# Transposing one more step by DMA, each transposition in two transfers, in a linear-attention and MLP kernel

## The chip, the cores and the metric

The kernel runs on one core of a Trainium2 chip. The metric is the device time of one execution in microseconds. Before the change it is 198.24 us, the median of three runs (198.15 to 199.05). The engines are named as in the profile: PE (TensorE, matrix products), PEld (its weight loads), DVE (VectorE), ACT (ScalarE), POOL (GpSimd) and SP (SyncE, which issues nearly all DMAs here; SPq is its queue of instructions).

## The reference

A lightning attention (linear attention with a decay `lam` per head) over 4 batches, 8 heads, 768 positions and head size 64, followed by a two-layer MLP with a tanh GELU (3072 tokens, 512 to 2048 to 512).

```python
for b in range(nb):                       # blocks of 64 positions
    intra = einsum('bhic,bhjc->bhij', qb, kb) * Dmask      # decayed causal mask
    intra = einsum('bhij,bhjd->bhid', intra, vb)
    inter = einsum('bhid,bhde->bhie', qb * lam_pow, kv_state)
    out[:, :, sl] = intra + inter
    kv_state = lam_block * kv_state + einsum('bhsd,bhse->bhde', kb * rev_pow, vb)
x = out.transpose(0, 2, 1, 3).reshape(3072, 512)
h = x @ w_in
g = gelu_tanh(h)
return g @ w_out
```

## The kernel before

**Steps.** The attention is cut into 24 steps. A step is one batch, one stretch of 256 positions and one half of the heads (four), so steps 2n and 2n + 1 are the two head halves of the same positions. For each step the kernel does the following, in functions that take the step's number:

- `load_step` (L60) issues the loads of q, k and v from HBM, 256 KB each, on SP (L70). The buffers rotate by four, so step n uses those of step n - 4.
- `cast_q` (L277) scales q by its decay into half precision on DVE (L282); `cast_k` (L290) casts k on ACT (L295); both write one tile `qk16`. `scale_v` (L264) scales v on POOL (L266). `prep_qk` is the casts and then `transpose_dma`; `prep` is `prep_qk` and then `prep_v`, which also issues loads for later steps.
- The scores need q and k with the head size on the partitions, so `qk16` is transposed into `qkT`. `FIRST_DMA_T` (L39) is 8. For steps below it `stage_t` (L309) transposes on PE (L321, eight instructions into one PSUM tile `Tps`), and ACT (L328, steps 5 and 6) or DVE (L330, steps 4 and 7) copies the result out. From step 8 on `transpose_dma` (L299) issues one transposing DMA on SP (L303) over queries and keys together, and `stage_t` returns at once.
- `scores` (L344) multiplies queries and keys on PE (L350); `causal` (L356) applies the mask on DVE (L360). `products` (L365) makes the products of keys and values of step n and the attention outputs of an earlier step s. `R(n, s)` (L967) is scores of n, products, mask and the first half of the state update; `U(n)` is the second half. `update` (L535) makes t on DVE (L547, L550) and u on POOL (L558, L565), and a later step's outputs read u.
- From step 13 on two steps at a time go through `burst` (L437).

**The MLP** follows in seven groups of positions. Its pieces are put in a list, `filler`, and `fill(n)` takes the next n pieces into PE's order. A piece is four or eight matrix products, of Hps (L613, first layer) or of MX, MY and MW (L692). The second layer uses sums of weight and activation blocks to save products; the sums of activations, gs (L662), are made on DVE behind the pieces that `queue_group` chose for them. The outputs of the MLP are put together on DVE (L734, L740), ACT (L714) and POOL (L749) and stored to HBM. The outputs of group 0 are kept in two tiles `o_pairs`, each stored by `store_pair` (L591) with two transfers on SP (L594). These tiles and the output tile of group 2 share two rotating buffers (tag `o32`), so that of group 2, first written at L734, takes over the buffer of pair 0.

**Order.** Every engine works its instructions off in the order in which the program names them (`pin`). The end of the function (from L993) is that order written out by hand, for all engines at once. A DMA waits on SP for its data and its buffer, and everything behind it on SP waits too. The change lies in the part from step 6 to step 12:

```python
    fill(1); prep(8); fill(1)            # L1076 to L1078
    stage_t(7)                           # L1079
    sum_wout(1, 4, DVE)
    fill(2)
    R(7, 6, lambda: prep_qk(9))          # L1082
    store_pair(0)
    U(7)
    scale_v(9)
    fill(2)
```

The loads run ahead of this: steps 0 to 8 are loaded by the opening of the function, step 9 by `prep(6)`, q and k of step 10 by `prep(7)`, step 11 by `prep(8)`, and v of step 10 behind step 9's transposition. The loop over `FILL` (L1088) then treats steps 8 to 12: in turn n it casts and transposes step n + 2 and issues the loads of later steps.

Of the kernel before, what the change touches and what calls it, by code (L numbers as in the profile page):

```python
# [15 lines left out]
def kernel(  # L16
# [10 lines left out]
    nc = tc.nc  # L27
    pin = tc.keep_in_program_order
# [7 lines left out]
    NF = DFF // P  # L36
    NC = DM // P
    NSTEP = B * NSB * 2
    FIRST_DMA_T = 8  # L39
    PSUM = bass.MemoryType.PSUM  # L40

    const = ctx.enter_context(tc.tile_pool(name="const", bufs=1))
# [17 lines left out]
    def load_step(s, names="qkv"):  # L60
        b, r = divmod(s, 2 * NSB)
        sb, half = divmod(r, 2)
        ts = ld32.setdefault(s, [])
        for nm, src in (("q", q), ("k", k), ("v", v)):
            if nm not in names:
                continue
            t = ld.tile([P, HH, 2, D], FP32, tag=nm + "32", name=f"{nm}32_{s}")
            rows = src[b, half * HH : (half + 1) * HH, sb * SB : (sb + 1) * SB, :]
            queue = nc.scalar if (nm, s) == ("v", 0) else nc.sync
            pin(queue.dma_start(out=t[:].rearrange("p h j d -> p h (j d)"),  # L70
                                in_=rows.rearrange("h (p j) d -> p h (j d)", j=2)))
            ts.append(t)
# [49 lines left out]
    def sum_wout(j, m, eng):  # L122

        a, op, b = W_SUMS[m]
        r = slice(4 * j, 4 * j + 4)

        def rows(t):
            if t in w_slot:
                return w_sum16[:, w_slot[t], r, :]
            f, e = t  # L130
            return w_out16[:, f * HF + r.start : f * HF + r.stop, e * HE : e * HE + HE]

        pin(eng.tensor_tensor(rows(m), rows(a), rows(b), op))
# [36 lines left out]
    def load_ahead(s):  # L170
        if s < NSTEP:
            load_step(s)
# [72 lines left out]
    def prep(s):  # L245
        prep_qk(s)
        prep_v(s)

    def wide(t):
        return t.rearrange("p j h d -> p h j d")  # L250

    def decay(t, s):
        hs = halves[s % 2]
        return t[:, hs, :].unsqueeze(3).to_broadcast([P, HH, 2, D])

    def prep_v(s):
        scale_v(s)
        if s >= 6:
            if s + 3 == FIRST_DMA_T + 2:
                load_step(s + 3, "qk")  # L260
            else:
                load_ahead(s + 3)

    def scale_v(s):  # L264
        tv = a16p.tile([P, 2, HH, D], FP16, tag="v16", name=f"v16_{s}")
        pin(nc.gpsimd.tensor_tensor(wide(tv[:]), ld32[s][2][:], decay(dv, s), ALU.mult))  # L266
        a16[s] = a16[s] + (tv,)

    def prep_qk(s):
        cast_qk(s)  # L270
        transpose_dma(s)

    def cast_qk(s):
        cast_q(s)
        cast_k(s)

    def cast_q(s):  # L277
        q32 = ld32[s][0]
        tqk = a16p.tile([P, 2, 2, HH, D], FP16, tag="qk16", name=f"qk16_{s}")
        tq, tk = tqk[:, 0], tqk[:, 1]  # L280
        q_eng = nc.gpsimd if s == 3 else nc.vector
        pin(q_eng.tensor_tensor(wide(tq), q32[:], decay(dq, s), ALU.mult))  # L282
        if s == 0:
            inverse(halves[0])
            odd(halves[1])
            inverse(halves[1])
        a16[s] = (tq, tk)
        whole_qk[s] = tqk
# [10 lines left out]
    def transpose_dma(s):  # L299
        tqk = whole_qk.pop(s)  # L300
        if s >= FIRST_DMA_T:
            o = qkp.tile([P, 2, 2, 2, P], FP16, tag="qkT", name=f"qkT_{s}")
            pin(nc.sync.dma_start_transpose(out=o[:].rearrange("p a j h t -> p (a j h) t"),  # L303
                                            in_=tqk[:].rearrange("p a j h d -> p (a j h d)")))
            qkT[s] = o
            if s == FIRST_DMA_T + 1:
                load_step(s + 1, "v")

    def stage_t(s):  # L309
        if s >= FIRST_DMA_T:  # L310
            return
        tq, tk = a16[s][:2]
        if s < 4:
            Tps = [ps_M.tile([P, 2, 2, P], FP16, tag="M", name=f"Tps{i}") for i in range(2)]
        else:
            Tps = ps_M.tile([P, 2, 2, 2, P], FP16, tag="M", name="Tps")
        for i, t in enumerate((tq, tk)):
            to = Tps[i] if s < 4 else Tps[:, i]
            for hp in range(2):
                for j in range(2):  # L320
                    pin(nc.tensor.transpose(to[:, j, hp, :], t[:, j, 2 * hp : 2 * hp + 2, :],  # L321
                                            ident[:]))
        o = qkp.tile([P, 2, 2, 2, P], FP16, tag="qkT", name=f"qkT_{s}")
        if s < 4:
            pin(nc.scalar.activation(out=o[:, 0], in_=Tps[0][:], func=AF.Copy))
            pin(nc.vector.tensor_copy(out=o[:, 1], in_=Tps[1][:]))
        elif s in (5, 6, 8):
            pin(nc.scalar.activation(out=o[:], in_=Tps[:], func=AF.Copy))  # L328
        else:
            pin(nc.vector.tensor_copy(out=o[:], in_=Tps[:]))  # L330
        qkT[s] = o
# [12 lines left out]
    def scores(n):  # L344
        o = qkT[n]
        Sps = [ps_M.tile([P, 2, 2, P], FP32, tag="M", name=f"S{hl}") for hl in range(2)]
        for hp in range(2):
            for jk in range(2):
                for hl, c in TILES:
                    pin(nc.tensor.matmul(  # L350
                        Sps[hl][half64(c), hp, jk, :], o[half64(hl), 1, jk, hp, half64(c)],
                        o[half64(hl), 0, :, hp, half64(c)], start=True, stop=True,
                        skip_group_check=True))
        Ss[n] = Sps

    def causal(n):  # L356

        t = ptp.tile([P, 2, 2, 2, P], FP16, tag="PT", name=f"PT_{n}")
        for hl, Sps in enumerate(Ss.pop(n)):
            pin(nc.vector.tensor_tensor(  # L360
                t[:, hl].rearrange("p b c d -> p b (c d)"), Sps[:].rearrange("p b c d -> p b (c d)"),
                mask[:].unsqueeze(1).to_broadcast([P, 2, 2 * P]), ALU.mult))
        PTs[n] = t
# [227 lines left out]
    def store_pair(pair):  # L591
        rows = out[2 * pair * P : 2 * pair * P + 2 * P, :].rearrange("(i p) d -> p i d", p=P)
        for i in range(2):
            pin(nc.sync.dma_start(out=rows[:, i], in_=o_pairs[pair][:, i]))  # L594
# [368 lines left out]
    def fill(n):  # L963
        for _ in range(min(n, len(filler))):
            filler.pop(0)()

    def R(n, s, ahead=None, keep=False):  # L967

        def first():
            if n is not None:  # L970
                scores(n)
            if ahead:
                ahead()

        if s in NARROW:
            products(n, s, between=first)
        else:
            first()
            products(n, s)
        if n is not None:  # L980
            causal(n)
        if s is not None and s % 2 == 1:
            g, i = group_of[s // 2]
            if i == len(groups[g]) - 1 and g > 0:
                queue_group(g)
        if n is not None and not keep:
            update(n, 0)

    def U(n):
        update(n, 1)  # L990
# [8 lines left out]
    R(0, None)  # L999
    idle(0, 384)  # L1000
    stage_t(1)
    idle(3)
    U(0)
# [72 lines left out]
    fill(1)  # L1076
    prep(8)
    fill(1)  # L1078
    stage_t(7)  # L1079
    sum_wout(1, 4, DVE)  # L1080
    fill(2)
    R(7, 6, lambda: prep_qk(9))  # L1082
    store_pair(0)
    U(7)
    scale_v(9)
    fill(2)

    FILL = {8: (2, 0, 0, 0), 9: (1, 2, 1, 2), 10: (0, 1, 1, 3), 11: (0, 1, 1, 3), 12: (0, 2, 1, 3)}  # L1088
    for n, (a, b, c, d) in FILL.items():
        stage_t(n)  # L1090
        fill(a + (n == 10))
        if n == 8:
            cast_q(n + 2)
            fill(1)
            cast_k(n + 2)
            transpose_dma(n + 2)
        else:
            prep_qk(n + 2)
        if n < 11:
            load_step(n + 4, "qkv" if n < 10 else "qk")  # L1100
        if n == 11:
            scale_v(13)
            load_step(14, "v")
            load_step(16, "qk")
        elif n == 9:
            scale_v(11)
        elif n == 10:
            scale_v(12)
            load_step(15, "qk")
        elif n == 12:  # L1110
            scale_v(14)
        fill(b + (n == 8) - (n == 10))
        R(n, n - 1, keep=n == 8)
        fill(c)
        if n == 8:
            update(n, 0)
            scale_v(n + 2)
            fill(2)
        U(n)
        if n == 12:  # L1120
            prep_qk(15)
            load_step(15, "v")
            load_step(16, "v")
            scale_v(15)
        fill(d)
        if n > 8:
            sum_win((n - 7) // 2, (n - 1) % 2, nc.vector)
# [40 lines left out]
    fill(1)  # L1168
    prep_qk(21)
    prep_v(20)  # L1170
    fill(3)

# [52 lines left out]
```

## Time and profile before

| what | value |
|---|---|
| time, median of three runs | 198.24 us (198.15 to 199.05) |
| profiled execution: its time, and its span | 198.35 us, 196.5 us |
| granted clock of PE | 1.000 |
| DVE busy | 145.7 us (74%) |
| DMA engines, busy share, 0 to 126 us | full or nearly in most slices |
| DMA_TRANSPOSE on SP | 16, of 1.23 to 3.36 us each on SP; 4.1 to 6.0 us from issue to landing, median 4.6 |
| loads of q, k and v | 256 KB each, median 4.9, 5.1 and 5.3 us from issue to landing |

The span runs from the first to the last instruction. The table of DMA issues gives the time from the start of an issue on SP to the landing of the last byte. In the chain of waits a piece is one stretch of equal instructions with its start, its length and its count; matrix products are pipelined, so lengths in the chain are counted up to the start of the next piece. In the timeline of SP a row is the issue of a DMA, not its transfer; the transfer goes on after it.

### The profile page before, as it was taken

The numbers are of one execution on the slowest core, as the hardware profiler recorded it, in microseconds if no ns is written. First come the engines' busy times: TensorE is split into PE (matmuls) and PEld (weight loads), VectorE is DVE, ScalarE is ACT, GpSimd is POOL, SyncE is SP. The second block draws the span as 40 slices with busy tenths as digits, with TensorE's granted clock in tenths as the row PEclk, the third lists the DMA queues.
The fourth block names the chain that finished last, engine by engine and source line by source line (L and its number), as shares of the span: only waits on it lengthen the run. The fifth ranks groups of instructions, "written<-read, shape, count | busy, mean of one in ns | idle before, by whom it ended". The sixth has DMA issues, their size and how long they took to land.

```text
span 196.5 us, 5993 instructions
## 1 busy us (share of the span) xinstructions
PE 190.4 (97%) x2467; PEld 139.2 (71%) x2469; DVE 145.7 (74%) x291; ACT 125.7 (64%) x248; POOL 68.5 (35%) x85
## 2 busy tenths in 40 slices
PE   8979999999999999999999999999999999999993
PEld 2556544456888888754688754578888888888882
DVE  4897722888989879959989826999557996487620
ACT  3663878358774796676856379844877856679221
POOL 6594213457444832528523416064002030002000
PEclk9999999999999999999999999999999999999999
DMA  5999999999999999989999999900520300020205
GB/s 166 291 323 385 384 385 386 302 293 276 267 218 239 262 199 220 239 137 220 361 240 273 251 333 164 227 6 0 36 95 32 110 5 0 3 107 31 79 15 198
DMA packets 62810, 38.13 MB, mean 194 GB/s; under 512 B 18624, under 2 KB 55744, under 8 KB 62784
## 3 DMA queue, kind: packets, MB, share of 16 engines
q1 hardware_dynamic: 62240, 37.50, 76.1%
q8 instruction: 19, 0.31, 0.6%
q10 hardware_dynamic: 544, 0.26, 0.5%
q14 instruction: 7, 0.06, 0.1%
HBM read 27.26 MB, written 6.29 MB: 171 GB/s over the span
## 4 chain that ended last, share of the span: by engine, by line
PE 89%; SPq 4%; DMA 4%; ACT 0%; issue 0%
PE Hps L613 25%; PE MX L692 18%; PE MY L692 9%; PE HX L796 7%; PE O2ps L628 7%; PE MW L692 4%; DMA wi<-in_moe_w_in_dram 4%; SPq L70 4%; PE HY L796 4%; PE S L350 3%; PE Hps L895 3%; PE HW L796 2%; PE O L460 1%; PE OK L400 1%; PE Tps L321 1%; PE OK L422 1%
## 5 line engine op out<-in xcount | busy, mean ns | idle before, releaser
L613 PE MATMUL Hps<-xT,w_in 128*128 128x512 f16 (+1 forms) x288 | 50.5, 332 | 0.0
L613 PEld LDWEIGHTS <-w_in 128*128 128x128 f16 x288 | 27.8, 98 | 19.4
L617 ACT ACTIVATE gT<-Hps 128x512 f16<-128x512 f32 x56 | 32.6, 597 | 9.2 <-PE Hps L613 8.7
L360 DVE TENSOR_TENSOR PT<-S,mask 128x512 f16<-128x512 f32 x48 | 30.3, 681 | 8.8 <-PE S L350 8.8
L266 POOL TENSOR_TENSOR v<-v,dv 128x512 f16<-128x512 f32 x24 | 27.4, 1147 | 19.9 <-DMA v<-in_v_dram 11.5
L692 PEld LDWEIGHTS <-gs 128*128 128x128 f16 x320 | 31.1, 98 | 3.7
L692 PEld LDWEIGHTS <-gT 128*128 128x128 f16 x240 | 23.1, 98 | 3.5 <-ACT gT L617 0.2
L565 POOL TENSOR_TENSOR u<-t,lumask 128x256 f16<-128x256 f32 x21 | 15.6, 758 | 22.1 <-DVE t L550 13.0
L692 PE MATMUL MX<-w_sum,gs 128*128 128x256 f16 x160 | 21.4, 273 | 0.0
L295 ACT ACTIVATE qk<-k 128x512 f16<-128x512 f32 x23 | 14.4, 625 | 7.3 <-DMA k<-in_k_dram 7.1
L282 DVE TENSOR_TENSOR qk<-q,dq 128x512 f16<-128x512 f32 x23 | 17.9, 780 | 1.1 <-DMA q<-in_q_dram 1.1
L749 POOL TENSOR_TENSOR o<-u,q 128x512 f32<-128x512 f32 (+1 forms) x5 | 5.6, 1120 | 37.3 <-issue 34.8
L662 DVE TENSOR_TENSOR gs<-gT 128x1024 f16<-128x1024 f16 (+1 forms) x24 | 16.4, 689 | 3.0 <-ACT gT L617 3.0
L558 POOL TENSOR_TENSOR u<-t,lamu 128x128 f16<-128x128 f32 x19 | 11.2, 597 | 18.7 <-DVE t L550 8.9
L628 PE MATMUL O2ps<-w_out,gT 128*128 128x512 f16 x64 | 14.6, 379 | 0.0
L796 PEld LDWEIGHTS <-ws 128*128 128x128 f16 x128 | 12.4, 98 | 1.7 <-DVE xs L775 0.3
L529 ACT ACTIVATE xT<-OK 128x256 f16<-128x256 f32 x22 | 8.7, 454 | 6.4 <-PE OK L413 3.1
L714 ACT ACTIVATE u<-MX 128x256 f32<-128x256 f32 x18 | 6.9, 383 | 7.4 <-PE MX L692 7.4
L628 PEld LDWEIGHTS <-gT 128*128 128x128 f16 x64 | 6.1, 98 | 6.6
L692 PE MATMUL MY<-w_out,gs 128*128 128x256 f16 x80 | 10.7, 273 | 0.0
L810 DVE COPY u<-HX 128x512 f32<-128x512 f32 x8 | 5.5, 689 | 6.8 <-ACT gT L814 4.4
L350 PEld LDWEIGHTS <-qkT 64*64 64x64 f16 x384 | 6.3, 106 | 5.8 <-issue 2.8
(105 smaller groups left out, 328.5 us busy)
## 6 DMA issues: line engine op xcount, KB each, us to landing
q<-in_q_dram SPq DMA_DIRECT2D x24, 256.0 KB, 4.9
k<-in_k_dram SPq DMA_DIRECT2D x24, 256.0 KB, 5.1
v<-in_v_dram SPq DMA_DIRECT2D x23, 256.0 KB, 5.3
out_dram<-o SPq DMA_DIRECT2D x23, 256.0 KB, 4.5
wo<-in_moe_w_out_dram SPq DMA_DIRECT2D x4, 1024.0 KB, 9.5
wi<-in_moe_w_in_dram SPq DMA_DIRECT2D x4, 512.0 KB, 8.1
wi<-in_moe_w_in_dram SPq DMA_DIRECT2D x2, 1024.0 KB, 13.8
v<-in_v_dram ACTq DMA_DIRECT2D x1, 256.0 KB, 4.3
```

The source lines that it names most:

```text
L266: pin(nc.gpsimd.tensor_tensor(wide(tv[:]), ld32[s][2][:], decay(dv, s), ALU.mult))
L282: pin(q_eng.tensor_tensor(wide(tq), q32[:], decay(dq, s), ALU.mult))
L295: pin(nc.scalar.activation(out=wide(tk), in_=k32[:], func=AF.Copy))
L350: pin(nc.tensor.matmul(Sps[hl][half64(c), hp, jk, :], o[half64(hl), 1, jk, hp, half64(c)], o[half64(hl), 0, :, hp, half64(c)], start=True, ...
L360: pin(nc.vector.tensor_tensor(t[:, hl].rearrange("p b c d -> p b (c d)"), Sps[:].rearrange("p b c d -> p b (c d)"), mask[:].unsqueeze(1).t ...
L565: pin(nc.gpsimd.tensor_tensor(u[:], state[half][:].unsqueeze(2).to_broadcast([P, 2, 2, D]), lumask[:, 2 * half : 2 * half + 2, :].unsqueez ...
L613: pin(nc.tensor.matmul(by_block(Hps[:, i, :]), w_in16[:, c, f * P : (f + 1) * P], x(c), start=(c == 0), stop=(c == NC - 1)))
L617: pin(nc.scalar.activation(out=dst, in_=Hps[:], func=AF.Gelu_apprx_tanh))
L628: pin(nc.tensor.matmul(O2[tau][0][:], gT[:, f % HF, f // HF, tau * P : (tau + 1) * P], w_out16[:, f, :], start=(n == 0), stop=(n == NF - 1)))
L662: pin(nc.vector.tensor_tensor(g_rows(m, i), g_rows(a, i), g_rows(b, i), op))
L692: pin(nc.tensor.matmul(dst, lhsT, rhs, start=(opens and i == 0), stop=(closes and i == HF - 1), skip_group_check=True))
L796: pin(nc.tensor.matmul(dst[:, i, :], w_in_block(a, slice(c, c + 1), slice(f * P, f * P + P))[:, 0], x_block(b, slice(c, c + 1))[:, 0], sta ...
```

## The change

Step 7 is transposed by DMA, too. Each transposition by DMA is two transfers, one of queries and one of keys. Step 9's loads are issued behind step 7's transposition, and q and k of step 10 and all of step 11 behind step 8's. Step 9 is cast behind update 7 instead of inside R(7, 6), and one fill piece goes from behind update 7 to ahead of R(7, 6). `store_pair(0)` is issued behind step 12's transposition. In turn 8 of the loop one fill piece goes from behind the key cast of step 10 to ahead of it.

```diff
-    FIRST_DMA_T = 8
+    FIRST_DMA_T = 7
...
     def prep_v(s):
         scale_v(s)
-        if s >= 6:
-            if s + 3 == FIRST_DMA_T + 2:
-                load_step(s + 3, "qk")
-            else:
-                load_ahead(s + 3)
+        if s == 8:
+            load_step(s + 2, "qk")
+        if s > 7:
+            load_ahead(s + 3)
...
             o = qkp.tile([P, 2, 2, 2, P], FP16, tag="qkT", name=f"qkT_{s}")
-            pin(nc.sync.dma_start_transpose(out=o[:].rearrange("p a j h t -> p (a j h) t"),
-                                            in_=tqk[:].rearrange("p a j h d -> p (a j h d)")))
+            for a in range(2):
+                pin(nc.sync.dma_start_transpose(out=o[:, a].rearrange("p j h t -> p (j h) t"),
+                                                in_=tqk[:, a].rearrange("p j h d -> p (j h d)")))
             qkT[s] = o
-            if s == FIRST_DMA_T + 1:
+            if s == 7:
+                load_step(s + 2)
+            elif s == 9:
                 load_step(s + 1, "v")
...
-        elif s in (5, 6, 8):
+        elif s in (5, 6):
             pin(nc.scalar.activation(out=o[:], in_=Tps[:], func=AF.Copy))
...
     prep(8)
     fill(1)
-    stage_t(7)
     sum_wout(1, 4, DVE)
-    fill(2)
-    R(7, 6, lambda: prep_qk(9))
-    store_pair(0)
+    fill(3)
+    R(7, 6)
     U(7)
+    fill(1)
+    prep_qk(9)
     scale_v(9)
-    fill(2)
...
         if n == 8:
             cast_q(n + 2)
-            fill(1)
+            fill(2)
             cast_k(n + 2)
             transpose_dma(n + 2)
         else:
             prep_qk(n + 2)
+        if n == 10:
+            store_pair(0)
         if n < 11:
             load_step(n + 4, "qkv" if n < 10 else "qk")
...
-        fill(b + (n == 8) - (n == 10))
+        fill(b - (n == 10))
         R(n, n - 1, keep=n == 8)
```

## The prediction

> **What bounds the kernel now.** I read the page's busy rows first (PE 97% of a span of 196.5 us, granted clock full in all slices), then the chain that ended last in order of time, then the stretches of 4 to 12 us.
>
> ```profile
> PE 190.4 (97%) x2467; PEld 139.2 (71%) x2469; DVE 145.7 (74%) x291; ACT 125.7 (64%) x248; POOL 68.5 (35%) x85
> ```
>
> The chain around step 7 (start us, us, what):
>
> ```profile
> 49.44 0.87 PE Hps L613 x8
> 50.31 0.45 PE Tps L321 x8
> 50.76 1.75 PE Hps L613 x16
> 52.50 0.35 PE S L350 x16
> ```
>
> Each piece begins where the one before ends: 49.44 + 0.87 = 50.31, and so on. In the stretches from 18.4 to 193.3 us PE is idle for 0.10 us in all. So no stall is left on PE that this change could take away. What it can gain is PE work that disappears; what it can lose is every wait of PE that it creates. The question is therefore how much slack each late operand has.
>
> **What goes.** Step 7's eight transpositions (0.45 us, the second chain row) leave PE and nothing lies beside them there: gain 0.45 us. The copy of the result, a DVE L330 of 0.69 us at 50.79, goes too; DVE is not on the chain there, so I count nothing. The fill pieces around step 7 keep their total of six; one of 0.87 us moves from behind update 7 to ahead of step 7's scores. These therefore start at 52.50 - 0.45 + 0.87 = 52.92, and everything from step 8 on 0.45 earlier (step 8's scores at 58.76 - 0.45 = 58.31). The edit of the copy's engine list for step 8 has no effect, since that step already went by DMA.
>
> **What is added: 18 more transposing DMAs on SP** (17 steps in two halves against 16 whole). The rows of SP's timeline that price them:
>
> ```profile
> 50.81 1.76 SPq L303 DMA_TRANSPOSE qkT<-qk  x1
> 52.63 0.56 SPq L70 DMA_DIRECT2D q<-in_q_dram  x1
> ...
> 83.39 1.23 SPq L303 DMA_TRANSPOSE qkT<-qk  x1
> 84.73 1.28 SPq L70 DMA_DIRECT2D v<-in_v_dram  x1
> ...
> 87.82 1.57 SPq L303 DMA_TRANSPOSE qkT<-qk  x1
> ```
>
> The trace has no half transposition. A whole one takes SP at least 1.23 us, a plain load at best 0.45. Bounds of a half: 0.62 (all of it scales) to 1.23 (none does). I take 0.84 = 0.45 + half of 0.78, so a pair takes 1.68, 0.45 more than one whole. Part of this costs nothing: the load behind step 15's transposition took 1.28 instead of 0.5, because SP was held up by what the transposition had queued, and a longer issue eats out of that hold-up. A gain is possible too: the queries' half waits for DVE alone and may start while ACT still casts the keys.
>
> A rule speaks against the split. The Trainium skill, "DMA: Bandwidth & Descriptors", section "Rules for kernel authors", says to join many small transfers into one large one, and its fit for a DMA (made for the GpSimd path, section "Anatomy of one DMA") has some 2.0 us that don't depend on size. If a second half paid that again in series, an estimate from that page, step 16's transposition would land 2.0 us later and, after the slack below, cost 1.7 us: 199.6. The trace has four loads issued back to back at 71.66, 72.28, 72.83 and 73.38; the first two landed 3.2 and 3.6 us after issue, 1.0 us apart, so the fixed parts overlap. I take the row: no second fixed part.
>
> **Step 7's new path.** Before, SP was free for step 9's loads at 45.89; these now stand behind step 7's transposition. Its query cast on DVE ends at 47.01, the key cast on ACT at 47.72; step 8's transposition began 0.15 us after its casts, so the halves are issued at 47.16 and, behind the first, 48.0. Landing: steps 14 and 15 took 4.1 us from issue with little in flight, steps 9 and 10 5.6 us behind a full queue. From 48.0 that is 52.1 to 53.6, needed at 52.92. The last load in front (v of step 8, issued 45.02, 5.0 to landing) lands at 50.0, and step 8's transposition landed 1.0 us behind its last load (k of step 10, 54.3 to 55.3). That is nearest to the lower end: 52.1 to 52.4, slack 0.5 to 0.8. Cost zero, at worst 0.7.
>
> **What stands behind it.** Loads land 0.85 us apart in this stretch (q and k of step 9: 50.9, 51.7). Between k of step 10 (54.3) and q of step 11 (57.4) lie 3.1 us for one transposition and one load, so a transposition holds the queue for 2.3. The skill's "Advanced Engine Details and Errata", section "X-Bar Transpose (TRN2)", calls transposing DMAs as fast as regular ones; by it step 7 would add 0.85 and q of step 10 would be in time, by the row it is late. I take the row. In order:
> - Step 9's loads are issued at some 49 to 50.6 instead of 45.9 to 48.6. At 5.0 they land from 54.0 on; the cast of q9 now stands behind update 7, at some 55.5. No wait.
> - Step 8's transposition: halves at 50.8 and 51.7, landing 56.2 (4.5 as before) to 57.3 (5.6), needed 58.31. No cost; cover gone only if it took 6.6.
> - q10 is issued at 52.5 instead of 48.67, lands at 57.6; DVE wants it at 57.42 - 0.45 = 56.97. DVE waits 0.6, with g sums and step 8's mask (L360) queued behind it. The g sum behind it began at 58.45 after 0.35 us idle; it now starts 0.28 late. The g sum that PE reads in the product MY of 62.29 ended at 61.73, and its second half is read 0.44 into that product, at 62.73: 1.0 us of slack, 0.7 of it left. Hidden, unless q10 lands after some 58.3; then every 0.1 us costs 0.1, at most 0.6. k10 is cast two fill pieces later than q10, behind a copy that ends at 58.8; it lands at 58.2.
> - Step 9: casts end at about 56.2, halves issued 56.3 and 57.1, landing by 62.7; scores at 64.34 - 0.45 = 63.9. Step 10: second half at 59.6, landed 65.2, needed 68.3. v10 comes 0.6 to 1.5 late; POOL has the update product of step 9 behind it, done by about 66.5 and needed at 68.6.
>
> **The two stores** (0.97 us of SP at 57.96) move from ahead of step 10's transposition to behind step 12's. That frees the queue where it is full. Step 12's casts end at 69.64 - 0.45 = 69.2; its halves leave SP at 71.0 or so, the stores at 72.0. They must land before DVE L734 writes the same output buffer for group 2 (77.50, so 77.05 now). With 3.6 us (the loads of that moment) they land at 75.6, with 5.1 (these stores before) at 77.1. I take the first. If late, DVE L734 holds up the g sum behind it (77.83, ended 78.33), which PE reads half way into the MY product of 78.27, at 78.71: 0.4 us of slack, so even 77.1 costs nothing. Step 14's loads follow 0.5 us late; their casts are at 78.6 and 79.2, landing at 76.
>
> **Step 16 is the narrowest place.** It was issued at 87.82, behind step 15's transposition and four loads, and landed 5.8 later, at 93.62. PE began the scores of steps 15 and 16 at 93.62 and reached step 16's half 0.28 us later. Slack 0.28. SP's chain begins at step 15's cast on DVE, so it moves up by 0.45 with PE. Against that stand step 15's extra issue (0 to 0.45) and step 16's own (0 to 0.45): 0 to 0.9 later, less 0.28 slack, is a stall of 0 to 0.6. Because the load behind had 0.8 us of hold-up to give, I take 0.4, so 0.1 of stall. The others have more: step 15 lands at 87.5 for 93.6, step 17 at 101.7 for 103.4, step 18 at 110.5 for 116.3.
>
> **Sum** on the profiled execution's 198.35 us (span 196.5 and 1.85 around it): 198.35 - 0.45 + 0.1 = 198.0. The median of three is 198.24, 0.11 lower, which would give 197.9; I leave 198.0.
>
> **Rivals.**
> 1. *Operands land late around steps 7 to 10* (queue as full as for step 9). For it: the DMA rows are full until some 65 us, and a transposition of 2.3 us is put in. Against it: slacks of 0.5 to 2. Step 7 0.7 late plus q10 0.3: 198.35 - 0.45 + 1.0 = 198.9. Chance 20%.
> 2. *Slower: the halves cost SP as much as wholes*, 1.23 us each. Place: step 16, with steps 15 and 16 each 1.23 longer, so 2.5 late less 0.28: 2.2 us of PE idle at 93.4. Sum 198.35 - 0.45 + 2.2 = 200.1. It decides from a half of about 1.0 us, where the stall is 1.1 and the time 199.0; past 0.5% from about 1.15 us, or less where rival 1 adds to it. For it: the shortest transpositions all lie at 1.23 to 1.28, as a fixed cost would. Against it: a plain load of the same bytes takes 0.45, so what is more must come from the pieces, which halve. Chance 18%.
> 3. *The copy that leaves DVE frees more than PE's 0.45.* Against it: PE has no idle time there. To be 0.5% faster needs 1.0 us. Chance 2%.
>
> **Chances.** Changes within 0.5% (1.0 us) can't be told from none here. Forecast (197.6 to 198.4) 60%; rival 1 20%, nearly all within 0.5%; rival 2 18%, nearly all past it; rival 3 2%. Faster 0.03, same 0.76, slower 0.21. The range 197.6 to 199.6 leaves out the upper part of rival 2.
>
> **What would show it.** Right: 34 DMA_TRANSPOSE rows of 0.7 to 0.9 us where SP is unhindered; eight Tps L321 fewer; scores of step 7 without idle PE before them; POOL, DVE and ACT waits at 55 to 65 us that nobody on PE waits for. Wrong: PE idle before S L350 at about 53 (rival 1) or 93.4 (rival 2), or before MY L692 at 61 to 62.

## The result and the profile after

The changed kernel takes 203.51 us (median of six, 202.16 to 204.84) against 198.24 (median of six here, 198.15 to 199.05): the ratio is 1.0257, with a 95% interval of 1.0205 to 1.031. It is slower, where the prediction had 198.0 and a range up to 199.6. The profiled execution took 204.84 us, the slowest of the six, with a span of 203.0 us against 196.5 before, so its waits show the places better than the typical sizes. The ratios below leave out executions that took over 1.5% longer than the fastest of their kernel: one of the kernel with a small extra transposition, three of the four with v on ACT, and one of 682.24 us of the kernel split in all steps but 15 and 16.

From the page of the changed kernel, the busy row and the shares of the chain that ended last:

```profile
PE 193.1 (95%) x2461; PEld 139.1 (68%) x2461; DVE 146.2 (72%) x290; ACT 126.9 (62%) x248; POOL 68.8 (34%) x85
...
PE 73%; DMA 16%; SPq 5%; ACT 2%; DVE 1%; issue 1%; ACTq 0%
```

The chain now leaves PE: DMA holds 16% of it, where PE held 89% and DMA 4% before. PE's own timeline names the places. A row is start us, length us, line and operation, and in brackets PE's idle time before it and what ended that:

```profile
62.61 0.61 PE L694 MATMUL MY<-w_out,gs 128*128 128x256 f16 x4 [0.55 <-DVE gs L664]
...
69.94 0.30 PE L415 MATMUL OK<-qkT,u 64*64 64x128 f16 x7 [0.36 <-POOL u L560]
...
78.97 0.61 PE L694 MATMUL MX<-w_sum,gs 128*128 128x256 f16 x4 [0.24 <-DVE gs L664]
...
80.84 0.61 PE L694 MATMUL MY<-w_out,gs 128*128 128x256 f16 x4 [0.82 <-DVE gs L664]
...
89.97 0.42 PE L352 MATMUL S<-qkT 64*64 64x128 f16 x16 [0.22 <-DMA qkT<-qk]
...
98.75 0.42 PE L352 MATMUL S<-qkT 64*64 64x128 f16 x16 [2.12 <-DMA qkT<-qk]
```

These six waits are 4.3 us in all, where PE had none in this stretch before. The largest is that of the scores of step 16, for the transposition. The first four look as if they came from DVE and POOL, but DVE, POOL and ACT had waited for late loads before, as these rows of theirs show; at 62.61 a late load is only part of the wait (more of it below). The scores of step 7, at 52.71 in the chain, wait for nothing.

```profile
58.66 0.69 DVE L281 TENSOR_TENSOR qk<-q,dq 128x512 f16<-128x512 f32 x1 [0.32 <-DMA q<-in_q_dram]
...
65.54 1.04 POOL L265 TENSOR_TENSOR v<-v,dv 128x512 f16<-128x512 f32 x1 [3.26 <-DMA v<-in_v_dram]
...
74.78 0.63 ACT L294 ACTIVATE qk<-k 128x512 f16<-128x512 f32 x1 [0.30 <-DMA k<-in_k_dram]
```

The six waits are not the whole loss. From the scores of step 8 to those of step 17 PE takes 51.83 us (58.02 to 109.85) instead of 44.69 (58.69 to 103.38), 7.1 us more. Of what the 4.3 us leave, some 1.7 us is a lower granted clock behind the longest wait, an estimate from the windows in the last section (what the clock lacks of 1.00 in the four from 99 to 103 us, added up); the other 1.1 us or so is lost inside pieces, where the profile shows no wait.

The transposing DMA itself, from the view of its line, before and after (durations in ns, lowest/median/highest):

```profile
L303 SPq DMA_TRANSPOSE qkT<-qk x16: 1232/1622/3359, 50.8 to 139.2; - x16
```

```profile
L303 SPq DMA_TRANSPOSE qkT<-qk x34: 1190/1232/2631, 46.9 to 146.9; - x34
```

A half takes SP no less time than a whole took: the shortest is 1.19 us and the median 1.23, where the shortest whole had 1.23. What that does to SP's queue ahead of step 16, in SP's timeline:

```profile
83.78 6.05 SPq L303 DMA_TRANSPOSE qkT<-qk  x4
89.92 1.09 SPq L70 DMA_DIRECT2D v<-in_v_dram  x2
91.06 0.50 SPq L70 DMA_DIRECT2D q<-in_q_dram  x1
91.61 0.50 SPq L70 DMA_DIRECT2D k<-in_k_dram  x1
92.22 2.92 SPq L303 DMA_TRANSPOSE qkT<-qk  x2
```

Four halves (steps 14 and 15), four loads and the two halves of step 16 follow each other with some 0.1 us between the rows. The chain of waits shows the end of it, the second half of step 16 on its way from 93.51 to 98.71 while PE is done with its piece at 96.6 or so:

```profile
91.11 2.40 PE Hps L615 x12
93.51 5.20 DMA qkT<-qk
98.71 0.04 issue
98.75 0.42 PE S L352 x16
```

### The profile page after: what moved, and what is told of

The parts are those of the page before. It is cut to its first block, busy times and chain, and to the rows that moved or that the text cites. A ratio compares the mean times of both kernels' runs of the same rounds, so it can differ in the third digit from the quotient of the medians.

```text
span 203.0 us, 6016 instructions
## 1 busy us (share of the span) xinstructions
PE 193.1 (95%) x2461; PEld 139.1 (68%) x2461; DVE 146.2 (72%) x290; ACT 126.9 (62%) x248; POOL 68.8 (34%) x85
## 4 chain that ended last, share of the span: by engine, by line
PE 73%; DMA 16%; SPq 5%; ACT 2%; DVE 1%; issue 1%; ACTq 0%
PE Hps L615 17%; PE MX L694 15%; DMA qkT<-qk 8%; PE MY L694 7%; PE HX L798 7%; PE O2ps L630 7%; DMA k<-in_k_dram 4%; SPq L70 4%; DMA wi<-in_moe_w_in_dram 4%; PE HY L798 4%; PE MW L694 3%; PE Hps L897 3%; PE S L352 2%; PE HW L798 2%; PE O L462 1%
## 5 line engine op out<-in xcount | busy, mean ns | idle before, releaser
L615 PE MATMUL Hps<-xT,w_in 128*128 128x512 f16 (+1 forms) x288 | 51.6, 337 | 0.0
L265 POOL TENSOR_TENSOR v<-v,dv 128x512 f16<-128x512 f32 x24 | 28.3, 1183 | 29.4 <-DMA v<-in_v_dram 20.7
L567 POOL TENSOR_TENSOR u<-t,lumask 128x256 f16<-128x256 f32 x21 | 14.8, 717 | 20.9 <-DVE t L552 11.8
L664 DVE TENSOR_TENSOR gs<-gT 128x1024 f16<-128x1024 f16 (+1 forms) x24 | 17.0, 715 | 5.8 <-ACT gT L619 5.8
L751 POOL TENSOR_TENSOR o<-u,q 128x512 f32<-128x512 f32 (+1 forms) x5 | 6.4, 1279 | 37.4 <-issue 34.8
L560 POOL TENSOR_TENSOR u<-t,lamu 128x128 f16<-128x128 f32 x19 | 10.7, 569 | 16.6 <-DVE t L552 6.0
L352 PE MATMUL S<-qkT 64*64 64x128 f16 x384 | 9.6, 221 | 3.1 <-DMA qkT<-qk 2.3
```

The source lines that it names most:

```text
L352: pin(nc.tensor.matmul(Sps[hl][half64(c), hp, jk, :], o[half64(hl), 1, jk, hp, half64(c)], o[half64(hl), 0, :, hp, half64(c)], start=True, ...
L567: pin(nc.gpsimd.tensor_tensor(u[:], state[half][:].unsqueeze(2).to_broadcast([P, 2, 2, D]), lumask[:, 2 * half : 2 * half + 2, :].unsqueez ...
L615: pin(nc.tensor.matmul(by_block(Hps[:, i, :]), w_in16[:, c, f * P : (f + 1) * P], x(c), start=(c == 0), stop=(c == NC - 1)))
L664: pin(nc.vector.tensor_tensor(g_rows(m, i), g_rows(a, i), g_rows(b, i), op))
```

## The experiments

Two theories at the start. **A**: an issue of DMA_TRANSPOSE costs SP some 1.2 us whatever its size; the split doubles the issues on a queue that had little slack. **B**: step 7 by DMA and the loads moved behind it overfill the DMA queue, and the split matters little.

### The split undone, and the split alone

The first kernel is the changed one with this edit; the second is the kernel before with the opposite edit.

```diff
-            for a in range(2):
-                pin(nc.sync.dma_start_transpose(out=o[:, a]..., in_=tqk[:, a]...))
+            pin(nc.sync.dma_start_transpose(out=o[:]..., in_=tqk[:]...))
```

> The changed kernel with one part undone: each transposition is one transfer again, of queries and keys together (17 of them, step 7 included). Theory A (a DMA_TRANSPOSE costs SP some 1.2 us whatever its size, and the split put 17 more of them on a queue that had little slack): 197.6 to 198.5 us, no wait of PE at the scores of step 16, transpositions of 1.23 us and more. Theory B (step 7 by DMA and the loads moved behind it fill the DMA queue; the split matters little): 201.5 us or more, with PE waiting at 60 to 62 and 78 to 81 us as in the changed kernel.

> The kernel before with only the split: steps 8 to 23 by DMA, in two transfers each; step 7 on PE, loads and stores in the old order. Theory A: 16 issues of 1.2 us more on SP; step 16 lands 2 us and more too late: 201.5 to 204 us. Theory B: 198.0 to 199.0 us.

Measured: whole, 198.51 us, ratio 1.0014 (0.9993 to 1.0035). Split alone, 201.22 us, ratio 1.015 (1.0109 to 1.0191). B falls: all that the change does besides the split costs nothing that can be told from zero. The parts don't add up, though: 0.14% and 1.5% against 2.6% together. In the profile of the split alone PE has exactly one wait between 44 and 160 us:

```profile
95.57 0.42 PE L351 MATMUL S<-qkT 64*64 64x128 f16 x16 [1.65 <-DMA qkT<-qk]
```

That is step 16, the narrowest place of the prediction. PE's last products (L692 before, L693 here, at 191.35 and 193.18) start 1.83 us later than before, that wait and little more. In the whole variant step 16 has no wait; the windows show 0.14 us of PE's idle time at 62 us, none else from 44 to 153 (a row is the stretch, its length, PE's busy time and so on):

```profile
62.00:63.00 1.00, 0.86 (x9) 0.63 (x8) 1.00 (x5) 0.67 (x2) 0.00 (x0) 1.00 2.78 241
```

### What sets the time of an issue

The kernel before, with a step cut into pieces where SP has nothing else to do. In the first, step 22 goes in two pieces of 512 columns and step 23 in four of 256; in the second, step 22 in 128 and 896 columns, and step 23 in two pieces of 64 rows and 1024 columns.

```diff
+            n = {22: 2, 23: 4}.get(s, 1)
+            for i in range(n):
+                w = 8 // n
+                pin(nc.sync.dma_start_transpose(out=dst[:, i * w : (i + 1) * w],
+                                                in_=flat[:, i * w * P : (i + 1) * w * P]))
```

> The kernel before with step 22 transposed in two transfers of 512 columns and step 23 in four of 256, where SP and the DMA queue have nothing else to do; steps 8 to 21 in one of 1024. Theory A: each transfer takes SP 1.2 us, so two take 2.5 and four take 4.9. If the issue scales with size (the prediction's 0.84 for a half): 0.8 for each half, 0.6 for each quarter. The time is 198.2 us either way, since step 22 is needed some 22 us later.

> The kernel before with step 23 transposed in two transfers of 64 rows and all 1024 columns, and step 22 in two of 128 rows with 128 and 896 columns. If the issue costs the same whatever is transposed: 1.2 us for each of the four (the second of a pair longer, as with two halves in a row). If it follows the rows: 0.6 to 0.8 us for the first of 64 rows, 1.2 us for that of 128 columns.

The first piece of step 22 and of step 23 in the first kernel (SP's timeline; the view of the line, in ns), and the first of step 22 in the second (SP's timeline):

```profile
125.38 1.20 SPq L308 DMA_TRANSPOSE qkT<-qk  x1
```

```profile
L308 SPq DMA_TRANSPOSE qkT<-qk x1: 1169/1169/1169, 139.2 to 139.2; - x1
```

```profile
125.69 1.13 SPq L312 DMA_TRANSPOSE qkT<-qk  x1
```

So 1.13 us for 128 columns, 1.17 for 256, 1.20 for 512 and 1.23 for 1024; the first piece of 64 rows took 1.20. Eight times the data costs 0.10 us more. At these sizes the issue is a fixed 1.1 us and next to nothing else. The second issue of a row of pieces took longer, 2.11 and 2.46 us (2.15 and 2.60 in the second kernel), the third and fourth 1.20 and 1.24 again.

### The number of issues without the split

Could it still be the halves, and not their number? The kernel before keeps its whole transpositions and gets a small extra one.

```diff
+            if s not in (8, 14, 20):
+                pin(nc.sync.dma_start_transpose(
+                    out=ident[:].unsqueeze(1),
+                    in_=tqk[:].rearrange("p a j h d -> p (a j h d)")[:, 0:P]))
             pin(nc.sync.dma_start_transpose(out=o[:]..., in_=tqk[:]...))
```

> The kernel before with one extra transposition of 128 columns (32 KB, the first block of the queries, into a tile that is no longer read) ahead of the whole one in 13 of the 16 steps (all but 8, 14 and 20). It moves an eighth more data, where the split moves none more, and adds an issue of 1.13 us per step, as the split does. If the number of issues on SP is what costs: PE waits for step 16 by 1.5 to 2.1 us, 200.3 to 202 us. If it is how the halves move their data: 198.2 to 199.0 us.

Measured: 201.06 to 202.21 us in three executions, ratio 1.0137 (1.0092 to 1.0183), as the split alone. Rows of its SP timeline and of PE's:

```profile
90.70 1.12 SPq L304 DMA_TRANSPOSE ident<-qk  x1
91.93 1.63 SPq L307 DMA_TRANSPOSE qkT<-qk  x1
```

```profile
97.00 0.42 PE L354 MATMUL S<-qkT 64*64 64x128 f16 x16 [1.55 <-DMA qkT<-qk]
```

An extra issue of 32 KB makes the same wait at the same place as the split of 256 KB in two. Is the transposition late because it moves its data more slowly, or because it starts later? The chains of this kernel and of the split alone have the last transfer of step 16:

```profile
91.93 5.03 DMA qkT<-qk
```

```profile
90.19 5.33 DMA qkT<-qk
```

From its issue to its landing it takes 5.0 and 5.3 us, and 5.2 in the changed kernel, no longer than the 5.8 us of the whole transposition before. It lands later because its issue starts later. A is shown by this: it is the issue, not the data. (The profiled execution is also 1.0 us late before the first extra issue, so its span is not compared; PE has one more wait there, 0.35 us at 79.15.)

### Where the issues hurt

Three kernels keep the split in some steps only. The edit is of this kind, with the condition as named in each expectation:

```diff
+            if s in (15, 16):          # or: s < 13
+                pin(nc.sync.dma_start_transpose(out=o[:]..., in_=tqk[:]...))
+            else:
                 for a in range(2): ...
```

> The changed kernel with steps 7 to 12 in one transfer each, and 13 to 23 in two. If the waits of PE at 60 to 82 us come from the issues of the early halves, which keep SP busy from step 7 on: they go, and what is left is step 16's wait as with the split alone, 200.5 to 201.3 us. If they come from step 7 by DMA and the moved loads: 202 us or more.

> The changed kernel with steps 15 and 16 alone in one transfer each. If the loss at step 16 is local (these two splits make it late): its 2.1 us wait of PE and the slow clock after it go, 199.5 to 200.5 us. If SP is behind from step 7 on, and what it lost before step 15 is carried on: 200.8 to 202.5 us, with a rest of that wait left.

> The kernel before with the split in all steps from 8 on but 15 and 16. In this order nothing was late before step 16 when all were split. If the loss of the split alone is made by the issues that stand directly ahead of step 16: its wait goes, 198.2 to 199.2 us, although 14 of 16 transpositions are still split. If it adds up over all the steps: 200 us or more.

Measured: early steps whole, 201.0 us, ratio 1.0126 (1.0068 to 1.0185), as expected. Its profile has the late waits at 95.50 and 127.61 and one of the earlier ones; so the waits at 60 to 82 us come for the most part from the issues of steps 7 to 12.

```profile
69.48 0.30 PE L419 MATMUL OK<-qkT,u 64*64 64x128 f16 x7 [0.34 <-POOL u L564]
95.50 0.42 PE L356 MATMUL S<-qkT 64*64 64x128 f16 x16 [1.09 <-DMA qkT<-qk]
127.61 0.42 PE L356 MATMUL S<-qkT 64*64 64x128 f16 x16 [0.59 <-DMA qkT<-qk]
```

The changed kernel with steps 15 and 16 whole: 203.2 us, ratio 1.0205 (1.0144 to 1.0267), which its interval doesn't separate from the changed kernel. Both expectations were too low. Step 16's wait falls to 0.68 us in its profile, but the waits ahead of it are there, and one of 1.0 us for step 9's scores is new.

With the kernel before and all split but 15 and 16: 198.54 to 200.78 us in four executions, ratio 1.0059 (1.0005 to 1.0112), between the two expectations; a fifth took 682.24 us, for which the record has no cause. In the profile, of the execution of 200.78 us, 0.38 us of wait is left at step 16, but two waits are new that the split alone does not have:

```profile
76.18 0.28 PE L697 MATMUL MX<-w_out,gT 128*128 128x256 f16 x1 [0.69 <-ACT gT L622]
79.21 0.61 PE L697 MATMUL MX<-w_sum,gs 128*128 128x256 f16 x4 [0.56 <-DVE gs L667]
```

ACT had waited 1.48 us for a load of k just before. So the three are 1.63 us in all, as much as the one wait of 1.65 in the profile of the split alone, only elsewhere. By the times, a part of the loss of the split alone goes with the issues directly ahead of step 16; how large a part is not settled, and the places of the waits change from one execution to another.

### The clock, and the loads of v on another queue

After its longest wait the changed kernel's PE ran at a lower granted clock. The first edit keeps PE busy with dummy products in that wait; the second takes nine loads off SP.

```diff
+        for _ in range(10 if n == 16 else 0):
+            pin(nc.tensor.matmul(Sps[0][:]..., ones[dt][:, 0:P], ones[dt][:], start=True, stop=True))
...
-            queue = nc.scalar if (nm, s) == ("v", 0) else nc.sync
+            queue = nc.scalar if nm == "v" and (s == 0 or 9 <= s <= 17) else nc.sync
```

> The changed kernel with ten dummy products of 512 columns on PE (some 2.2 us) ahead of the scores of step 16, where PE waits 2.1 us for the transposition. If a good part of the loss is the slow clock after that wait: 202.0 us or less, granted clock 1.0. If the wait alone counts: 203.0 to 204.0 us.

> The changed kernel with the loads of v for steps 9 to 17 issued by ACT instead of SP: the same transfers in the same DMA engines, some 4.5 us of issue off SP between 49 and 96 us. If SP's issue time is the limit: 200 to 202 us, with step 16's wait shorter by a microsecond or more. If the DMA engines' own throughput is the limit, or ACT is held up by its issues: 203 us or more.

Filling the wait: 203.89 us, ratio 1.0298 (1.0253 to 1.0343), no gain, with a full clock in the profile. The dummy products can cost PE time of their own, so this alone does not decide it; but two of the changed kernel's six executions, of 202.16 and 202.73 us, had a mean clock of 1.000 and were some 4 us slower than before all the same. The clock is not what makes the typical execution slow. The loads on ACT: the executions scattered from 200.62 to 206.71 us, too far apart for a ratio, and its profile has new waits of PE for the transpositions of step 7 (1.13 us) and at 91.88 (2.35 us). ACT itself was held up: it stood idle until a load in its own queue was issued.

```profile
91.91 0.37 ACTq L70 DMA_DIRECT2D v<-in_v_dram  x1
92.33 1.09 ACT L619 ACTIVATE gT<-Hps 128x512 f16<-128x512 f32 x2 [4.29 <-DMA qkT<-qk]
```

So the run has the second of the expected ends, for a reason that lies in ACT; it neither supports nor refutes A.

### A faster version?

The whole variant, with q of step 10 loaded ahead of step 8's transposition:

```diff
             if s == 7:
                 load_step(s + 2)
+                load_step(s + 3, "q")
...
         if s == 8:
-            load_step(s + 2, "qk")
+            load_step(s + 2, "k")
```

> The changed kernel with whole transpositions, and q of step 10 loaded ahead of step 8's transposition: PE's 0.14 us wait of the whole variant at 62 us should go, so that the eight transpositions that left PE are a gain: 197.6 to 198.0 us, 0.1 to 0.3% below the kernel before. If step 8's transposition then comes late, PE waits at 58 us and nothing is gained.

Measured: 198.78 us, ratio 1.0028 (1.0018 to 1.0038), a little slower. Its profiled execution has a span of 196.3 us, 0.2 below that before, but most of its executions lie near 198.8, and what they wait for was not profiled. The expectation was wrong in its place, too: in the profile DVE takes q of step 10 without a wait, and PE's idle 0.14 us at 62 us is still there. It has another cause (next section). No version here beats the kernel before.

## Why the prediction was wrong

**The step that failed** is "I take 0.84 = 0.45 + half of 0.78, so a pair takes 1.68". A half measured 1.19 us at its shortest and 1.23 in the median, and the shortest pair takes 2.5. The reasoning behind it was that a plain load of the same bytes takes 0.45 us, and that what a transposition takes more must come from the pieces and so halve. The pieces account for 0.10 us of it. The other row, "the shortest transpositions all lie at 1.23 to 1.28, as a fixed cost would", was in the rival and was the better evidence. What was right in this step: SP's hold-up behind step 15 did give way, since the two loads there took 1.09 us instead of 1.83; but 0.7 us back does not pay for two extra issues.

**Rival 2 had the mechanism and the place.** It put 2.2 us of idle PE at step 16; the changed kernel's profile has 2.12, the split alone 1.65. That the 2.12 comes so close is in part luck: when it occurs, SP is already 4.4 us behind the kernel before and PE's scores of step 15 are 2.7 us behind, neither of which the rival counted. Its time, 200.1, was too low for the change because it charged the issues at step 16 alone. Its thresholds don't follow from its own sum either: a half of 1.0 us gives a stall of 2 x 0.77 - 0.28 = 1.3 us, not 1.1, so 0.5% is passed from a half of some 1.0, not 1.15. The slacks at steps 7 to 12 had been worked out with 1.68 for a pair. With 2.5, SP is busy from 46.9 to 83.8 us with hardly a gap and falls behind: by 0.8 us at the transposition of step 8, 2.3 at step 10, 3.9 at step 13, against the kernel before. So q of step 10 was issued at 54.28 (52.5 in the prediction), the halves of step 9 at 57.7 and 59.4 (56.3 and 57.1). That is rival 1's mechanism, late operands around step 10, set off by rival 2's. The early steps whole (1.0126 against 1.0257) price it at about half of the loss.

**A second term, put at nothing**, was "the cast of q9 now stands behind update 7, at some 55.5. No wait." The cast was followed to its own operand only. It takes 0.75 us of DVE, and its new place is ahead of the g sums that PE reads at 62 us. DVE's rows of the cast and of that g sum before, and in the whole variant:

```profile
52.40 0.68 DVE L282 TENSOR_TENSOR qk<-q,dq 128x512 f16<-128x512 f32 x1
...
61.16 0.57 DVE L662 TENSOR_TENSOR gs<-gT,gs 128x512 f16<-128x512 f16 x1
```

```profile
55.18 0.75 DVE L281 TENSOR_TENSOR qk<-q,dq 128x512 f16<-128x512 f32 x1
...
61.67 0.57 DVE L663 TENSOR_TENSOR gs<-gT,gs 128x512 f16<-128x512 f16 x1
```

The g sum comes 0.5 us later, although PE asks for it 0.57 earlier (in the product MY at 61.56 instead of 62.13). In the whole variant the chain of waits runs on DVE alone from 54.8 us to this g sum and ends in PE's wait at 62 us, which is why an earlier q10 didn't remove it. No run puts the cast back, so this is read from the chain and not tested.

**Right**: PE's eight transpositions leave. In the whole variant PE takes 10.77 us from the scores of step 6 to those of step 8 instead of 11.21, 0.44 less, as predicted. But 0.32 of that is lost by the scores of step 9, at that g sum, and another 0.10 by those of step 11; in the times nothing can be seen of it. Step 7's halves, though 2.95 us on SP, were in time. So was the output buffer of pair 0: no wait for the two stores appears at L736 (L734 before). Late q10 was expected to be hidden; with the halves it makes DVE wait 0.32 us more on top of the cast, and both end in PE's 0.55 us wait at 62.61.

**The rule weighed.** The Trainium skill's "DMA: Bandwidth & Descriptors" advises to join small transfers ("Rules for kernel authors"). It was set aside because back-to-back loads overlap their fixed parts. They do in flight, and the halves need no longer there than the wholes (4.6 us from issue to landing, median of both); the fixed part that counts here is on SP, ahead of the flight, where one issue follows the other. The rule's advice was right for this change; the estimate from it, 199.6, was too low.

**Open**: why the parts add up to 1.6% and the whole change costs 2.6%. SP's lateness carried from the early halves to step 16 accounts for the direction, but the kernel meant to isolate it (15 and 16 whole in the changed order) gave no clear answer.

## What to carry to other kernels

Price a DMA on its issuing queue by count before pricing it by bytes: a transposing DMA here costs 1.1 to 1.2 us of SP per issue, 32 KB or 256 KB alike, and no split here made a kernel faster. Where one queue issues loads, transpositions and stores in a fixed order, look at the sum of its issues between two points where it is free, not at the slack of each operand on its own. When an instruction is moved, ask what it now stands ahead of, not only what it waits for itself. When two rows price an unseen operation differently, the row of the same operation (its shortest samples at one floor) counts for more than that of a relative.

## What the runs showed of the hardware

An issue on an idle queue directly behind another transposing issue took 2.1 to 2.6 us, but the third and fourth in a row took 1.2 again; in the changed kernel a pair took 2.5 us and more together. What holds the second one up was not tried.

PE's granted clock halved after a wait of 2.12 us. The windows of the changed kernel's profile (stretch, length, PE, PEld, DVE, ACT, POOL, then the clock, the DMA share and GB/s):

```profile
97.00:98.00 1.00, 0.00 (x0) 0.00 (x0) 1.00 (x3) 0.63 (x1) 1.00 (x3) 1.00 1.54 48
98.00:99.00 1.00, 0.25 (x17) 0.25 (x20) 0.32 (x1) 0.00 (x0) 0.09 (x1) 1.00 1.26 301
99.00:100.00 1.00, 1.00 (x78) 1.00 (x69) 0.55 (x1) 0.00 (x0) 0.27 (x1) 0.76 1.01 369
100.00:101.00 1.00, 1.00 (x16) 0.48 (x7) 1.00 (x4) 0.57 (x1) 0.77 (x1) 0.50 1.09 414
101.00:102.00 1.00, 1.00 (x3) 0.30 (x2) 1.00 (x4) 0.96 (x3) 0.73 (x2) 0.50 1.10 374
102.00:103.00 1.00, 1.00 (x4) 0.39 (x3) 1.00 (x3) 0.97 (x2) 0.40 (x1) 0.53 1.08 324
```

It was 1.00 again at 103 us. The Trainium skill's "TensorE: Matmul & The Clock Gate", section "Why this matters for your kernels", puts the limit at gaps of some 3 us; here 2.1 were enough in this execution, and in the profile of the loads of v on ACT the clock fell to 0.50 after the wait of 2.35 us, while the 1.65 us wait of the split alone left it at 1.00. Across the six executions the mean clock lay between 0.989 and 1.0, so this adds to some of them and not to all.
